# Fourier stage: own products in two halves, odd tokens' products on a summed tile, another order of the token tiles

## Chip, core and metric

The kernel runs on one core of a Trainium2 chip. The metric is the device time of one execution in microseconds (us), taken as the median of several runs. The engines are PE (TensorE, with PEld for its weight loads), DVE (VectorE), ACT (ScalarE), POOL (GpSimd) and SP (SyncE). In this trace each engine takes its own instructions in the order in which they stand (PE may load weights ahead), and they wait for one another by semaphores.

## The reference, cut to what matters

```python
def _attn_ref(q, k, v, proj):          # 2 x 8 heads x 768 tokens x 64
    mask = q_bucket[:, :, :, None] == k_bucket[:, :, None, :]
    ...
    return np.matmul(attn, v)
def _moe_ref(x, w_val, conv_w, w_out): # x: 2 x 768 x 512
    ...                                # gate: sigmoid of a 5-tap convolution along the tokens
    val = x @ w_val
    return gate * val @ w_out
def _moe2_ref(x, w_ch1, w_ch2):
    X = np.fft.fft(np.fft.fft(x, axis=1), axis=2)   # along tokens and along channels
    mixed = np.real(X)
    u = x + mixed
    un = (u - mu) / np.sqrt(var + 1e-06)            # layer norm over 512 channels
    ch = np.maximum(un @ w_ch1, 0.0) @ w_ch2        # 512 -> 2048 -> 512
    return u + ch
```

The change lies in the second half of `_moe_ref` (the product with `w_out`) and in the Fourier part of `_moe2_ref`.

## The kernel before

The program has three stages: attention (to about 245 us), the gated product and the Fourier part (`mixing`, to about 336 us), and the channel products (`channel`, to the end). The order of instructions on each engine is the order of the code: nothing is moved by a scheduler.

Each float32 number is split into a high and a low part of fewer bits, and a product is made of three: high by high, high by low, low by high. The Fourier part uses that a sequence of 768 splits into an even and an odd half of 384 (s = 0 and s = 1), each of three token tiles of 128 (kt = 0, 1, 2), for two batches b. That makes twelve jobs (b, s, kt). `mixing` is a software pipeline over rounds i = 0 to 13. In round i it runs

- `own` for job i: the product with `w_out`, 12 matmuls of 512 columns into one PSUM bank (4 channel blocks by 3 part products);
- `along_d` for job i-2: the transform along the channels, 6 matmuls of 258 columns for each part, then ACT writes the high part of the result into `ah` (tile `a` in the trace) and DVE the low part into `al`;
- `turn` for job i-1: two transposes, a copy on ACT (tile `ft`, high) and a subtraction on DVE (`ft`, low), which `along_d` of the next round reads;
- `fold` for job i: ACT copies the bank to a tile `y`, DVE folds it.

When all six jobs of a batch have gone through `along_d`, `both(b, kt)` runs `mixed` for s = 0 and 1 (the transform along the tokens: 9 matmuls of 258 columns over the three tiles, and then the odd tokens' extra products with the table `odd`), `total` (DVE adds the result to `y`) and two additions on GpSimd that give `u`. For batch 0 this stands in round 7, between `turn(6)` and round 8, for batch 1 behind round 13. The extra products are 2 for s = 0 (high and low of slot 3, of which row 0 alone counts), none for s = 1 with kt above 0, and 6 for s = 1 with kt = 0: the table's rows sum over all tokens, tile by tile, high and low. So a batch has 11 + 15 + 11 + 9 + 11 + 9 = 66 matmuls of 258 columns here.

Rounds 5 and 6 also hold the splitting of a 64-bit weight block for the channel stage (`channel_split`: DVE L146 to L157, ACT L149, L161, L169, GpSimd L162), rounds 8 to 10 the centering of `u[0]` (`center`), rounds 11 to 13 its transposes (`u_transpose`). The tiles `y` have seven buffers, so `fold` of job 7 waits until GpSimd has read a `y` of the first `both`.

Of the kernel before, what the change touches and what calls it, by code (L numbers as in the profile page):

```python
# [10 lines left out]
F32 = mybir.dt.float32  # L11
F32R = mybir.dt.float32r
AF = mybir.ActivationFunctionType
ALU = mybir.AluOpType
# [3 lines left out]
P = 128  # L18
B, H, S, D = 2, 8, 768, 64
DM = H * D  # L20
# [5 lines left out]
NC = DM // P  # L26
HS = S // 2
NL = 258
# [21 lines left out]
def dft_tables():  # L50


    d = np.arange(1, DM // 2 + 1)
    l = np.arange(NL)
    ang = 2.0 * np.pi * ((d[:, None] * l[None, :]) % DM) / DM
    cs = np.stack([np.cos(ang), np.sin(ang)], 0)
    cs[0, -1] = 0.5 - (l % 2)
    cs[1, -1] = 0.0
    ch, cl = split12(cs)
    wide = np.stack([ch, cl], 1).reshape(2, 2, 2, P, NL).transpose(3, 0, 1, 2, 4)  # L60

    j = np.arange(HS)
    k = np.arange(HS)
    ang = 2.0 * np.pi * ((j[:, None] * k[None, :]) % S) / S
    c = np.cos(ang)
    s = -np.sin(ang)
    c[0, 1::2] = 0.0
    c[1::2, 0] = 0.0
    s[:, 0] = 0.0
    t = 2.0 * np.stack([c, s], 0)  # L70
    th, tl = split12(t)
    seq = np.stack([th, tl], 1).reshape(2, 2, HS // P, P, HS).transpose(3, 0, 1, 2, 4)

    odd = np.zeros((P, 2, P), np.float32)
    odd[0, 0, 1::2] = 2.0
    odd[1::2, 1, 0] = 2.0
    return (
        np.ascontiguousarray(wide, dtype=np.float32),
        np.ascontiguousarray(seq, dtype=np.float32),
        odd,  # L80
    )
# [23 lines left out]
def block_kernel(  # L105
# [4 lines left out]
    nc = tc.nc  # L110

    def f32(ap):
        return ap.bitcast(F32)
# [922 lines left out]
    def u_transpose(b, t, psum):  # L1036
        pu = psum()
        for c in range(NC):
            nc.tensor.transpose(pu[:, c * P : (c + 1) * P], u[b][:, t, c * P : (c + 1) * P], ident)
        ts_ = slice(t * P, (t + 1) * P)  # L1040
        pv_ = pu.rearrange("p (c t) -> p c t", c=NC)
        nc.scalar.copy(uth[0][:, :, ts_], pv_)
        nc.vector.tensor_tensor(utl[0][:, :, ts_], pv_, f32(uth[0])[:, :, ts_], op=ALU.subtract)

    def mixing(es):
# [13 lines left out]
        gh, gl = {}, {}  # L1059
# [123 lines left out]

        def own(b, s, kt):
            yp = psum()
            n = 0
            for x, w in ((gh[b, s], wo_h), (gh[b, s], wo_l), (gl[b, s], wo_h)):
                for c in range(NC):
                    nc.tensor.matmul(  # L1189
                        yp, x[:, c, kt * P : (kt + 1) * P], w[c], start=n == 0, stop=n == 3 * NC - 1  # L1190
                    )
                    n += 1
            return yp

        ys, folds, turned = {}, {}, {}
# [23 lines left out]
        def along_d(b, s, kt, part):  # L1219
            fh, fl = turned[b, s, kt, part]  # L1220
            ops = [(x[:, i, :], tab[:, part, w, i, :]) for x, w in ((fh, 0), (fh, 1), (fl, 0)) for i in range(2)]
            pa = psum()
            for n, (x, w) in enumerate(ops):
                nc.tensor.matmul(pa[:, :NL], x, w, start=n == 0, stop=n == len(ops) - 1)  # L1224
            ah, al = sums[b]
            slot = kt if part == s else 3
            high, low = ah[:, part, slot, :], al[:, part, slot, :]
            if part:
                nc.scalar.copy(high, pa[:, :NL])
                nc.vector.tensor_tensor(low, pa[:, :NL], f32(high), op=ALU.subtract)  # L1230
            else:

                y0 = ys[b, s, kt][:, 0:1]
                nc.scalar.activation(high, pa[:, :NL], AF.Identity, bias=y0)
                nc.vector.scalar_tensor_tensor(
                    low, pa[:, :NL], y0, f32(high), op0=ALU.add, op1=ALU.subtract
                )

        def mixed(b, s, kt):
            ah, al = sums[b]  # L1240
            ks = slice(kt * P, (kt + 1) * P)
            ops = []
            for x, w in ((ah, 0), (ah, 1), (al, 0)):
                for jt in range(3):
                    ops.append((seq[:, s, w, jt, ks], x[:, s, jt, :]))
            if s == 0:
                ops += [(odd[:, 0, :], ah[:, 0, 3, :]), (odd[:, 0, :], al[:, 0, 3, :])]
            elif kt == 0:
                for jt in range(3):
                    ops += [(odd[:, 1, :], ah[:, 0, jt, :]), (odd[:, 1, :], al[:, 0, jt, :])]  # L1250
            pm = psum()
            for n, (w, x) in enumerate(ops):
                nc.tensor.matmul(pm[:, :NL], w, x, start=n == 0, stop=n == len(ops) - 1)  # L1253
            return pm
# [13 lines left out]
        def both(b, kt):  # L1268

            pm = [mixed(b, s, kt) for s in range(2)]  # L1270
            for s in range(2):
                total(b, s, kt, pm[s])
            for t, op in ((kt, ALU.add), (3 + kt, ALU.subtract)):
                nc.gpsimd.tensor_tensor(u[b][:, t, :], ys[b, 0, kt], ys[b, 1, kt], op=op)
# [14 lines left out]
        for i in range(len(jobs) + 2):  # L1289
            if i < len(jobs):  # L1290
                yp = own(*jobs[i])
            if i > 1:
                for x in spans(jobs[i - 2]):
                    if x[0] not in sums:
                        sums[x[0]] = [m2.tile([P, 2, 4, NL], F32R, tag=y, name="a") for y in ("ah", "al")]
                    along_d(*x)
            if 0 < i <= len(jobs):
                for x in spans(jobs[i - 1]):
                    turn(*x)
            if i == 7:  # L1300
                both(0, 0)
                both(0, 1)
            if i < len(jobs):
                fold(*jobs[i], yp)
            if i == 0:
                last_gates()
            elif i == 5:
                nc.scalar.activation(warm, warm, AF.Sqrt)
            if 0 < i < 5:
                for s in range(2):  # L1310
                    part_high(1, s, i - 1)
                    part_low(1, s, i - 1)
            if i < 4:
                even_odd(1, i)
            elif i == 4:
                gs.close()
                late_tiles()
                channel_load(0)
                channel_load(1)
            elif i == 7:  # L1320
                both(0, 2)
            elif 8 <= i < 11:
                for t in (i - 8, i - 5):
                    center(0, t)
            elif 5 <= i < 7:
                channel_split(i - 5)
            elif i > 10:
                for x in range(2):
                    u_transpose(0, 2 * (i - 11) + x, psum)
        wnext.extend(channel_steps(2, spare=False))  # L1330
        run(wnext.pop(0) for _ in range(3))
        both(1, 0)
        wnext.pop(0)()
        for kt in range(1, 3):
            both(1, kt)

    with ExitStack() as es:
# [127 lines left out]
```

## Time and profile before

| | us |
|---|---|
| median of 3 runs | 611.06 |
| lowest and highest | 610.6, 614.76 |
| the profiled execution's own time | 610.95 |
| its span | 609.1 |
| PE busy in the span | 600.7 |
| DVE, ACT, POOL busy | 441.4, 357.7, 265.3 |

The span is what the trace covers; the profiled execution's own time is 1.85 us longer. Rows of the trace give the start of an instruction, its duration, and for a matmul a modelled end. Consecutive matmuls overlap in the rows, so the pace of a stream is the distance of starts, not the duration of one.

### The profile page before, as it was taken

The numbers are of one execution on the slowest core, as the hardware profiler recorded it, in microseconds if no ns is written. First come the engines' busy times: TensorE is split into PE (matmuls) and PEld (weight loads), VectorE is DVE, ScalarE is ACT, GpSimd is POOL, SyncE is SP. The second block draws the span as 40 slices with busy tenths as digits, with TensorE's granted clock in tenths as the row PEclk, the third lists the DMA queues.
The fourth block names the chain that finished last, engine by engine and source line by source line (L and its number), as shares of the span: only waits on it lengthen the run. The fifth ranks groups of instructions, "written<-read, shape, count | busy, mean of one in ns | idle before, by whom it ended". The sixth has DMA issues, their size and how long they took to land.

```text
span 609.1 us, 10268 instructions
## 1 busy us (share of the span) xinstructions
PE 600.7 (99%) x3711; PEld 537.5 (88%) x3711; DVE 441.4 (72%) x849; ACT 357.7 (59%) x712; POOL 265.3 (44%) x274
## 2 busy tenths in 40 slices
PE   8999999999999999999999999999999999999997
PEld 7899999999999999998989888888888888888885
DVE  4999999999999997998679788988884411110113
ACT  5989999999999997745524455555665011111121
POOL 7251769788888798963341532332330000000000
PEclk9999999999999999999999999999999999999999
DMA  5967776878777712170200243443430200000002
GB/s 133 213 154 165 170 147 164 179 167 189 165 177 178 173 43 57 43 293 2 70 1 9 86 126 127 138 120 123 139 103 1 104 0 1 1 0 1 0 1 104
DMA packets 52556, 62.01 MB, mean 102 GB/s; under 512 B 28704, under 2 KB 39304, under 8 KB 52250
## 3 DMA queue, kind: packets, MB, share of 16 engines
q1 hardware_dynamic: 51770, 57.81, 37.3%
q0 software_dynamic: 432, 3.55, 1.5%
q8 instruction: 29, 0.48, 0.3%
q14 instruction: 21, 0.17, 0.1%
q10 hardware_dynamic: 304, 0.01, 0.0%
HBM read 36.73 MB, written 3.19 MB: 66 GB/s over the span
## 4 chain that ended last, share of the span: by engine, by line
PE 90%; DVE 6%; ACT 2%; issue 1%; DMA 1%; POOL 0%; SPq 0%; ACTq 0%; POOLq 0%
PE pf L1372 21%; PE acc L1382 20%; PE op L629 10%; PE sp L570 10%; PE ptp L606 9%; PE ps L1189 5%; PE ps L222 3%; PE ps L1253 3%; PE ps L1224 1%; PE bp L456 1%; PE late L222 1%; PE ptp L714 1%; PE early L222 1%; DVE ptl L618 1%; PE idle L369 1%
## 5 line engine op out<-in xcount | busy, mean ns | idle before, releaser
L1382 PE MATMUL acc<-w,hid 128*128 128x512 f32 x576 | 137.4, 391 | 0.0
L1382 PEld LDWEIGHTS acc<-w,hid 128*128 128x128 f32 x576 | 105.5, 188 | 20.1
L1375 DVE SCALAR_TENSOR_TENSOR hid<-pf,hid 128x512 fp32r<-128x512 f32 (+1 forms) x62 | 33.4, 556 | 120.6 <-ACT hid L1374 120.6
L1372 PE MATMUL pf<-uth,w 128*128 128x512 f32 (+1 forms) x496 | 97.2, 337 | 0.1
L1374 ACT ACTIVATE hid<-pf 128x512 fp32r<-128x512 f32 (+1 forms) x62 | 28.9, 488 | 114.9 <-PE pf L1372 114.9
L581 DVE TENSOR_SCALAR_CACHE_REDUCE sd<-sp 128x768 f32<-128x768 f32 x96 | 91.0, 948 | 4.8 <-PE sp L570 3.1
L618 DVE TENSOR_TENSOR ptl<-ptp,pth 128x768 fp32r<-128x768 f32 x96 | 91.5, 953 | 2.3 <-ACT pth L614 2.0
L570 PE MATMUL sp<-qk 128*128 128x512 f32 (+1 forms) x384 | 91.1, 359 | 1.7 <-DVE sd L581 0.8
L1372 PEld LDWEIGHTS pf<-uth,w 128*128 128x128 f32 x496 | 78.8, 188 | 15.6 <-DVE hid L1375 1.8
L588 ACT ACTIVATE sd<-sd,nm 128x768 f32<-128x768 f32 x96 | 90.5, 942 | 1.5 <-DVE sd L581 1.5
L614 ACT CAST pth<-ptp 128x768 fp32r<-128x768 f32 x96 | 77.4, 806 | 13.6 <-PE ptp L714 5.7
L162 POOL TENSOR_TENSOR w<-cv 128x512 fp32r<-128x512 f32 x31 | 40.4, 1302 | 89.0 <-DVE cv L157 74.5
L606 PE MATMUL ptp<-ident,sd 128*128 128x128 f32 x576 | 78.5, 272 | 0.2 <-ACT sd L588 0.2
L629 PE MATMUL op<-ptl,v 128*128 128x256 f32 x288 | 73.3, 284 | 0.2 <-DVE ptl L618 0.2
L629 PE MATMUL op<-pth,v 128*128 128x256 f32 x288 | 73.3, 282 | 0.0
L606 PEld LDWEIGHTS ptp<-ident,sd 128*128 128x128 f32 x576 | 65.8, 140 | 1.1 <-ACT sd L588 0.5
L570 PEld LDWEIGHTS sp<-qk 128*128 128x128 f32 x384 | 58.2, 189 | 8.3 <-DVE sd L581 1.6
L629 PEld LDWEIGHTS op<-pth,v 128*128 128x128 f32 x288 | 54.1, 188 | 4.1
L629 PEld LDWEIGHTS op<-ptl,v 128*128 128x128 f32 x288 | 54.1, 188 | 0.6 <-DVE ptl L618 0.4
L1372 PE MATMUL pf<-utl,w 128*128 128x512 f32 (+1 forms) x248 | 53.1, 335 | 0.0
L241 POOL TENSOR_TENSOR g<-g,conv_tmp 128x768 f32<-128x768 f32 x27 | 46.5, 1723 | 1.6
L149 ACT ACTIVATE cv<-cv,col 128x512 int32<-128x512 int32 x32 | 23.2, 725 | 40.4 <-DVE cv L146 40.4
(214 smaller groups left out, 984.2 us busy)
## 6 DMA issues: line engine op xcount, KB each, us to landing
raw<-in_moe_w_ch_dram SPq DMA_DIRECT2D x32, 512.0 KB
qk<-ht SPq DMA_DIRECT2D x60, 192.0 KB
qk<-lt SPq DMA_DIRECT2D x30, 192.0 KB
rqk<-in_q_dram SPq DMA_DIRECT2D x16, 192.0 KB
rqk<-in_k_dram SPq DMA_DIRECT2D x16, 192.0 KB
rv<-in_v_dram SPq DMA_DIRECT2D x8, 384.0 KB
out_dram<-o SPq DMA_DIRECT2D x12, 256.0 KB
xm<-xc SPq DMA_DIRECT2D x15, 192.0 KB
```

The costliest lines, as they stand in the source:

```text
L162: nc.gpsimd.tensor_tensor(dst()[1], fold(g.bitcast(F32)), fold(e.bitcast(F32)), op=ALU.mult)
L241: nc.gpsimd.tensor_tensor(dst, dst, tmp, op=ALU.add)
L570: nc.tensor.matmul(sp[:, cs], q2[i][:, m, qi * P : (qi + 1) * P], k2[i][:, m, cs], start=m == order[0], stop=m == order[1])
L581: nc.vector.tensor_scalar(sd[n], sp, CLAMP, None, op0=ALU.min, op1=ALU.min, accum_out=st[p]["nm"][:, n % 12 : n % 12 + 1],)
L588: nc.scalar.activation(sd[n], sd[n], AF.Exp, bias=st[p]["nm"][:, i : i + 1], scale=-1.0, accum_out=st[p]["sums"][:, i : i + 1],)
L606: nc.tensor.transpose(tp[:, r // 3, c0 : c0 + P], sd[n][:, r * P : (r + 1) * P], ident)
L614: nc.scalar.copy(p_parts(n)[0], tp)
L618: nc.vector.tensor_tensor(lo, tp, f32(ho), op=ALU.subtract)
L629: nc.tensor.matmul(po[kb], v3[:, r, c0 : c0 + P], pt[kb][x][:, r, :], start=r == 0 and x == 0, stop=r == R - 1 and x == 1,)
L1372: nc.tensor.matmul(pf, w[:, c, :], x[:, c, cs], start=n == 0, stop=n == 3 * NC - 1)
L1375: nc.vector.scalar_tensor_tensor(hl[:, cs], pf, 0.0, f32(hh)[:, cs], op0=ALU.max, op1=ALU.subtract)
L1382: nc.tensor.matmul(acc, x[:, ts_], w, start=f == 0 and n == 0, stop=f == NF - 1 and n == 2)
```

## The change

- `own` makes its bank in two halves of 256 columns, each a group of 12 matmuls: 24 matmuls where 12 were. `fold` still waits for the whole.
- For s = 0 the extra products are one matmul instead of two: DVE writes the low part of row 0 to row 32 of the high tile's slot 3, and the table `odd` has a second row of twos there.
- For s = 1 and kt = 0 they are two instead of six: GpSimd adds the high and low tiles of s = 0 over kt into `tot` (three additions behind `along_d` of kt = 1, two behind that of kt = 2), ACT copies the sum into the high tile's unused slot, and GpSimd subtracts to get its low part.
- `both` runs in the order kt = 1, 2, 0, and `center` and `u_transpose` of batch 0 follow that order.

```diff
+    odd[32, 0, 1::2] = 2.0
...
         def own(b, s, kt):
             yp = psum()
-            n = 0
-            for x, w in ((gh[b, s], wo_h), (gh[b, s], wo_l), (gl[b, s], wo_h)):
-                for c in range(NC):
-                    nc.tensor.matmul(
-                        yp, x[:, c, kt * P : (kt + 1) * P], w[c], start=n == 0, stop=n == 3 * NC - 1
-                    )
-                    n += 1
+            for c0 in range(0, DM, 2 * P):
+                n = 0
+                for x, w in ((gh[b, s], wo_h), (gh[b, s], wo_l), (gl[b, s], wo_h)):
+                    for c in range(NC):
+                        nc.tensor.matmul(
+                            yp[:, c0 : c0 + 2 * P], x[:, c, kt * P : (kt + 1) * P], w[c][:, c0 : c0 + 2 * P],
+                            start=n == 0, stop=n == 3 * NC - 1,
+                        )
+                        n += 1
             return yp
...
+                rows = slice(0, 1 if s else P)
                 nc.vector.scalar_tensor_tensor(
-                    low, pa[:, :NL], y0, f32(high), op0=ALU.add, op1=ALU.subtract
+                    high[32:33] if s else low, pa[rows, :NL], y0[rows], f32(high)[rows], op0=ALU.add, op1=ALU.subtract
                 )
+                if s == 0 and kt:
+                    all_tokens(b, kt)
+
+        tokens = {}
+
+        def all_tokens(b, kt):
+            ah, al = (f32(x) for x in sums[b])
+            oh = sums[b][0][:, 1, 3, :]
+            if kt == 1:
+                tokens[b] = m2.tile([P, NL], F32, tag="tot", name="tot")
+            t = tokens[b]
+            add = [ah[:, 0, kt, :], al[:, 0, kt, :]]
+            if kt == 1:
+                add.append(al[:, 0, 0, :])
+            for n, x in enumerate(add):
+                nc.gpsimd.tensor_tensor(t, ah[:, 0, 0, :] if kt == 1 and n == 0 else t, x, op=ALU.add)
+            if kt == 2:
+                nc.scalar.copy(oh, t)
+                nc.gpsimd.tensor_tensor(sums[b][1][:, 1, 3, :], t, f32(oh), op=ALU.subtract)
...
             if s == 0:
-                ops += [(odd[:, 0, :], ah[:, 0, 3, :]), (odd[:, 0, :], al[:, 0, 3, :])]
+                ops.append((odd[:, 0, :], ah[:, 0, 3, :]))
             elif kt == 0:
-                for jt in range(3):
-                    ops += [(odd[:, 1, :], ah[:, 0, jt, :]), (odd[:, 1, :], al[:, 0, jt, :])]
+                ops += [(odd[:, 1, :], x[:, 1, 3, :]) for x in (ah, al)]
...
             if i == 7:
-                both(0, 0)
                 both(0, 1)
+                both(0, 2)
...
             elif i == 7:
-                both(0, 2)
+                both(0, 0)
...
-                for t in (i - 8, i - 5):
+                for t in ((i - 7) % 3, (i - 7) % 3 + 3):
                     center(0, t)
...
-                    u_transpose(0, 2 * (i - 11) + x, psum)
+                    u_transpose(0, (1, 4, 2, 5, 0, 3)[2 * (i - 11) + x], psum)
...
-        both(1, 0)
+        both(1, 1)
         wnext.pop(0)()
-        for kt in range(1, 3):
+        for kt in (2, 0):
             both(1, kt)
```

Lines after the change carry other numbers: L1214 is then L1217, L1199 is L1202, L1229 is L1232, L1234 is L1237, L149, L161, L162 and L169 one more each.

ACT in rounds 6 and 7 of the kernel before, from the high part of job 4 to that of job 5 (`a` high part, `ft` the turned tile of job 5, `y` job 6, `cv` and `w` the split of a weight block):

```order
L1234 ACTIVATE a<-ps,y 128x258 [waits PE_49,Activation_49]
L1214 CAST ft<-pw 128x256 [waits PE_49]
L1199 COPY y<-ps 128x512
L149 ACTIVATE cv<-cv,col 128x512 [waits DVE_49,Activation_49]
L161 ACTIVATE cv<-cv 128x512 [waits DVE_49,Pool_49]
L169 CAST w_0_4176<-cv 128x512 [waits DVE_49]
L1229 CAST a<-ps 128x258 [waits PE_49]
```

The same stretch of ACT in the changed kernel:

```order
L1237 ACTIVATE a<-ps,y 128x258 [waits PE_49,Activation_49]
L1259 CAST a<-tot 128x258 [waits Pool_49]
L1217 CAST ft<-pw 128x256 [waits PE_49]
L1202 COPY y<-ps 128x512
L150 ACTIVATE cv<-cv,col 128x512 [waits DVE_49,Activation_49]
L162 ACTIVATE cv<-cv 128x512 [waits DVE_49]
L170 CAST w_0_4240<-cv 128x512 [waits DVE_49]
L1232 CAST a<-ps 128x258 [waits PE_49]
```

The copy of the sum, which waits for GpSimd, now stands ahead of the copy of `ft` and of all that follows; in round 12 it stands in the same way between the high part of job 10 and the copy of `ft` of job 11.

POOL in rounds 4 to 7 of the kernel before, from the last pair of low parts of the gated tiles (`gl`) to the first `u`:

```order
L1090 TENSOR_TENSOR gl<-gt_3963,gh 128x384 [waits Activation_49]
L1090 TENSOR_TENSOR gl<-gt_3964,gh 128x384 [waits Activation_49]
L162 TENSOR_TENSOR w_0_4175<-cv 128x512 [waits DVE_49,Activation_49]
L162 TENSOR_TENSOR w_0_4177<-cv 128x512 [waits DVE_49,PE_49,Activation_49]
L1274 TENSOR_TENSOR u_4161<-y 128x512 [waits DVE_49]
```

The same stretch of POOL in the changed kernel:

```order
L1257 TENSOR_TENSOR tot<-tot,a 128x258 [waits DVE_49,Pool_49]
L1257 TENSOR_TENSOR tot<-tot,a 128x258 [waits Pool_49]
L1091 TENSOR_TENSOR gl<-gt_3963,gh 128x384 [waits Activation_49]
L1091 TENSOR_TENSOR gl<-gt_3964,gh 128x384 [waits Activation_49]
L163 TENSOR_TENSOR w_0_4239<-cv 128x512 [waits DVE_49,Activation_49]
L1257 TENSOR_TENSOR tot<-tot,a 128x258 [waits Activation_49,Pool_49]
L1257 TENSOR_TENSOR tot<-tot,a 128x258 [waits DVE_49,Pool_49]
L1260 TENSOR_TENSOR a<-tot,a 128x258 [waits DMAHW5_49,Activation_49]
L163 TENSOR_TENSOR w_0_4241<-cv 128x512 [waits DVE_49,PE_49,Activation_49]
```

The additions of kt = 1 stand ahead of the last `gl` pair, those of kt = 2 behind the first weight block of the channel stage, and the subtraction behind ACT's copy.

## Rows read from the trace of the kernel before

**Rows 1.** The page: its first line, and busy time by engine (share, instructions).

```profile
span 609.1 us, 10268 instructions
PE 600.7 (99%) x3711; PEld 537.5 (88%) x3711; DVE 441.4 (72%) x849; ACT 357.7 (59%) x712; POOL 265.3 (44%) x274
```

**Rows 2.** The page's chain that ended last, shares of the span by engine.

```profile
PE 90%; DVE 6%; ACT 2%; issue 1%; DMA 1%; POOL 0%; SPq 0%; ACTq 0%; POOLq 0%
```

**Rows 3.** Windows: stretch, length, then PE, PEld, DVE, ACT, POOL busy, clock.

```profile
320.00:330.00 10.00, 9.85 (x74) 9.06 (x73) 9.73 (x23) 5.77 (x15) 0.00 (x0) 1.00 0.00 1
```

**Rows 4.** Chain in order of time: start, length, piece, instructions.

```profile
269.79 5.61 PE ps L1189 x24
...
299.02 8.21 PE ps L1253 x66
...
328.06 7.95 PE ps L1253 x66
```

**Rows 5.** Timeline of PE, channel stage: start, duration, line, shapes, count.

```profile
487.88 1.08 PE L1372 MATMUL pf<-uth,w 128*128 128x256 f32 x8
488.79 0.62 PE L1372 MATMUL pf<-utl,w 128*128 128x256 f32 x4
489.25 4.26 PE L1382 MATMUL acc<-w,hid 128*128 128x512 f32 x18
```

**Rows 6.** Chain in the attention stage: groups of six 256-column matmuls.

```profile
62.68 0.70 PE op L629 x6
```

**Rows 7.** The page's groups: weight loads of the channel stage's first product.

```profile
L1372 PEld LDWEIGHTS pf<-uth,w 128*128 128x128 f32 x496 | 78.8, 188 | 15.6 <-DVE hid L1375 1.8
```

**Rows 8.** Timeline of PE, round 7 and the first `both`.

```profile
297.92 0.88 PE L1224 MATMUL ps<-tab,ft 128*128 128x258 f32 x6
298.64 0.38 PE L1209 MATMUL pw<-ident,fold 128*128 128x128 f32 x2
298.78 1.33 PE L1253 MATMUL ps<-a,seq 128*128 128x258 f32 x9
...
300.19 1.49 PE L1253 MATMUL ps<-a,seq 128*128 128x258 f32 x9
...
307.06 2.01 PE L1189 MATMUL ps<-qk,gh 128*128 128x512 f32 x8
```

**Rows 9.** Timeline of ACT, rounds 6 and 7, and round 12.

```profile
295.91 0.47 ACT L1234 ACTIVATE a<-ps,y 128x258 fp32r<-128x258 f32 x1
296.28 0.36 ACT L1214 CAST ft<-pw 128x256 fp32r<-128x256 f32 x1
296.53 0.60 ACT L1199 COPY y<-ps 128x512 f32<-128x512 f32 x1
...
300.14 0.37 ACT L1229 CAST a<-ps 128x258 fp32r<-128x258 f32 x1
...
324.94 0.49 ACT L1234 ACTIVATE a<-ps,y 128x258 fp32r<-128x258 f32 x1
325.32 0.38 ACT L1214 CAST ft<-pw 128x256 fp32r<-128x256 f32 x1
```

**Rows 10.** Timeline of POOL, rounds 4 to 6.

```profile
289.39 1.98 POOL L1090 TENSOR_TENSOR gl<-gt,gh 128x384 fp32r<-128x384 f32 x2 [1.90 <-ACT gh L1087]
295.95 1.29 POOL L162 TENSOR_TENSOR w<-cv 128x512 fp32r<-128x512 f32 x1 [4.59 <-DVE cv L157]
```

**Rows 11.** Timeline of PE, round 13: `along_d` of job 11.

```profile
325.80 0.72 PE L1224 MATMUL ps<-tab,ft 128*128 128x258 f32 x4
326.68 0.51 PE L1224 MATMUL ps<-tab,ft 128*128 128x258 f32 x2 [0.15 <-DVE ft L1215]
```

**Rows 12.** Timeline of DVE: the fold of round 6, the low part in round 12.

```profile
297.16 0.42 DVE L1202 TENSOR_TENSOR fold<-ps,y 128x256 f32<-128x256 f32 x1
...
325.81 0.48 DVE L1235 SCALAR_TENSOR_TENSOR a<-ps,y,a 128x258 fp32r<-128x258 f32 x1
```

## The prediction, made before the changed kernel was run

> **What bounds the kernel now.** I read the page's first lines, then the chain that ended last, then windows and timelines of the stretch that the change touches. The page [rows 1] shows PE busy for 600.7 of 609.1 us, and the chain [rows 2] puts 90% of the span on PE. In the Fourier stage PE starts one matmul behind another without a gap that counts: even in the window from 320 to 330 us, where DVE is nearly full as well, PE is busy 9.85 of 10 us, at full granted clock [rows 3]. So in this stage two things move the end: how long PE's streams take, and any wait that is put into them. GpSimd is idle in that window, and all that the change gives it lies beside PE, unless somebody waits for it. Who waits is the question of this prediction.
>
> **Streams on PE: own products.** The chain gives 5.61 us for 24 matmuls of 512 columns [rows 4], 233.8 ns each and 2.805 us for a bank. No row shows these products in halves. The nearest is the channel stage's first product, which also runs twelve matmuls of 256 columns with new weights each into one bank: they start at 487.88 us, the next stream at 489.25 [rows 5], so 1.37 us for twelve and 114 ns each. Two halves are then 2.74 us, 0.065 us less than one whole. Over twelve banks that is 12 x 0.065 = 0.78 us gained. Other rows bound it from the other side: six matmuls of 256 columns in attention take 0.70 us [rows 6], 117 ns each, and a bank 2.80 us, so nothing gained; 66 matmuls of 258 columns take 7.95 us [rows 4], 120.5 ns each, and at that pace a bank costs 2.89 us, 0.085 us more, 1.0 us lost in all. I take the row of the channel stage, whose twelve steps into one bank are the same form, and keep 1.0 us lost as the other end.
>
> The Trainium skill, "TensorE: Matmul & The Clock Gate", section "Back-to-back issue gap", gives 262 cycles for 256 columns and 518 for 512 at full clock: by it two halves cost 6 cycles, 2.5 ns, more than a whole, 0.36 us over 144 pairs, where the rows above give 228 against 234 ns. It speaks against the change, and by it the sum below would be 1.1 us higher. The trace does not bear out its pace for the whole (216 ns against 234 ns).
>
> **Streams on PE: odd tokens.** For each batch s = 0 drops one matmul for each of three tiles, and s = 1 drops four: seven of 120.5 ns, 0.84 us, 1.69 us for both. These stand in the middle of the stream and all of it is PE's path. The changed order of tiles adds and removes no matmul; the transposes and the centering only follow it. The single-row write to row 32 replaces a DVE instruction of the same length along the columns; I cost it at nothing, since DVE's instruction stays in its place.
>
> If nothing waited, the sum would be 0.78 + 1.69 = 2.47 us gained.
>
> **What GpSimd's additions cost by themselves.** Two pairs of rows bound one addition of 258 columns: 384 columns take 1.98 / 2 = 0.99 us, 512 columns 1.29 us [rows 10]. The straight line through both gives 0.70 us for 258, in proportion to columns it would be 0.67; 0.99 is the upper end. I take 0.71. The three behind kt = 1 are waited for by nobody soon: GpSimd idles 1.90 us ahead of the `gl` pair [rows 10], so they push that pair by at most one addition, and the banks of batch 1 read it last among their part products. I cost them at nothing; if that cover were gone it would be one addition, 0.7 us, once.
>
> **The new wait, batch 0.** The copy of the sum stands in ACT's queue ahead of the copy of `ft` of job 5, and waits for GpSimd. Behind it are queued, in this order, the copy of `ft`, the copy `y` of job 6, three steps of a weight block's split, and the high part of job 5. In the kernel before ACT began the high part of job 4 at 295.91, `ft` at 296.28, `y` at 296.53, the high part of job 5 at 300.14 [rows 9]. PE began `along_d` of job 5, which reads `ft`, at 297.92 [rows 8]: it had the copy (0.36 us long) 1.3 us ahead.
>
> Now the steps, by the clock of the kernel before. Six banks come ahead of round 6, so all is 6 x 0.065 = 0.39 us earlier there. GpSimd ends the weight block at 295.95 + 1.29 - 0.39 = 296.85 [rows 10] and only then begins the first addition; two end at 298.27. ACT's copy starts at 298.29, `ft` 0.25 us behind it (the distance between `ft` and `y` in the rows) at 298.54, and is done 0.37 us later, at 298.91. PE is there at 297.92 - 8 x 0.065 = 297.40. **First wait: 1.5 us.** `along_d` lasts 0.72 us (297.92 to 298.64 [rows 8]), to 299.63. Meanwhile `y` starts at 298.79, 2.26 us later than before, and with it the fold of job 6, which ends at 297.16 + 0.42 + 2.26 = 299.84 [rows 12]: 0.2 us more until PE's transposes. They take 0.14 us; then ten matmuls for s = 0 and two for s = 1, 12 x 0.1205, bring PE to 301.43. The third one for s = 1 reads the high part of job 5, which stands behind the split in ACT's queue: the whole chain fold, DVE's split steps, ACT's split steps is 2.26 us later, so it is ready at 300.14 + 2.26 + 0.37 = 302.77. **Second wait: 1.35 us.** From there 7 + 19 + 21 = 47 matmuls, 5.66 us, end at 308.43, where the next bank starts. In the kernel before it started at 307.06 [rows 8]. So batch 0 is 1.37 us later: waits of 1.5 + 0.2 + 1.35 = 3.05, less 0.52 of eight banks, 0.84 of odd tokens, and 0.3 that the mixing lost before (8.28 us from 298.78 to 307.06 for 66 x 0.1205 = 7.95 [rows 4, 8]).
>
> The second `both` now mixes kt = 2 before job 7's fold can have its `y`, but no bank or tile runs out for PE by the order of the changed kernel: the fold would be done at about 309, and its transposes come behind the next bank and `along_d`, at about 312.
>
> **Between.** Four banks, 4 x 0.065 = 0.26 us, earlier.
>
> **The new wait, batch 1.** In round 12 the same copy stands between the high part of job 10 (324.94) and `ft` of job 11 (325.32) [rows 9]. GpSimd is idle there, so the first addition starts at once and ends at 324.94 + 0.49 + 0.71 = 326.14; the second needs DVE's low part, done at 325.81 + 0.48 = 326.29 [rows 12], and ends at 327.01. Copy at 327.03, `ft` at 327.28, done at 327.66, where PE began `along_d` of job 11 at 325.80 and its last two at 326.68 [rows 11]. It would end at 327.66 + 0.72 = 328.38 in place of 326.68 + 2 x 0.12 = 326.92. **Third wait: 1.46 us** more than before. Against it stand the 0.84 us of odd tokens: 0.62 us later at the end of the mixing. GpSimd's subtraction (0.71 us behind ACT's copy) is read by the last matmul of the mixing, some 8 us later, and hidden. The channel stage begins with weights and `u` that were ready before, and DVE's totals keep their distance to PE, so I carry the delay through to the end.
>
> **Sum.** 1.37 - 0.26 + 0.62 = 1.73 us later, against the profiled execution's own time of 610.95, 0.11 us under the median: 612.7 us. The gain of 2.47 us is more than paid back by 4.5 us of waits, less 0.3 that goes away.
>
> **Rivals.** *The gain is had.* ACT's wait is hidden, because GpSimd is sooner done than I price it or PE has other work. For it: GpSimd is idle in batch 1 and PE waits for nearly nothing now. Against it: in round 12 `ft` was done at 325.70 and PE began at 325.80, so a delay of over 0.1 us shows, and in round 6 (done at 296.65, begun at 297.92) one of over 1.3 us. Then 2.47 us are gained: 608.5 us. Chance 0.18.
>
> *Halves cost more than wholes.* At 120.5 ns a bank costs 0.085 us more in place of 0.065 less, 12 x 0.15 = 1.8 us: 614.5 us, and with additions of 0.99 us (two in each of two waits, the first counted twice, 0.28 x 2 + 0.28 = 0.85 us) 615.4. It decides from 117 ns a matmul on, and is slower than before on any count. For it: the rows of 258 columns. Against it: twelve in a row at 114 ns. Chance 0.17.
>
> *Weight loads set the pace of halves.* One load lasts 188 ns [rows 7], and halves need 288 of them, 54.1 us where 144 wholes took 33.7. If a load stopped hiding behind a matmul of 256 columns, 20.4 us would come on top: 633 us, slower by over 3%. It decides where the pace goes over 117 ns towards 188. Against it: the channel stage's 256-column products need the same load for each matmul and run at 114 ns. Chance 0.03.
>
> *The change does nothing*, waits and gains cancelling within 0.5 us: part of the forecast's lower end, 611 us; chance 0.04.
>
> **How the numbers follow.** My forecast, three waits against two gains, has 0.58: 612.7 us. The range must take in the gain that is had and the dear halves, since each alone has almost 0.2: from 608.4 to 615.4 us. What a measurement of this kernel can tell from no change is about 1%, 6.1 us. Only the weight loads, and noise beyond what three runs show, reach that: slower by over 1% 0.04, faster by over 1% 0.02, within it 0.94.
>
> **What would show it.** In the profile after, ACT should show a wait of some 2 us ahead of the copy of the sum in rounds 6 and 12, released by GpSimd; PE should show waits of about 1.5 us ahead of `along_d` of jobs 5 and 11 and about 1.3 us in the first `mixed` for s = 1, where the kernel before has 0.15 us in job 11 [rows 11] and none that counts elsewhere. A bank of own products should take 2.74 us. The extra products should leave 59 matmuls of 258 columns in each mixing. PE's waits absent, or a bank at 2.8 us or more, would each show a step wrong; a granted clock under full behind one of the waits would make all of it wrong.

## The result, and the profile after

The changed kernel takes 615.5 us (median of 19 runs, 614.1 to 618.23), the kernel before 611.1 us (19 runs). The ratio is 1.0071, with a 95% interval from 1.0061 to 1.0081: 4.4 us slower, where 1.7 us were forecast. The profiled execution took 615.5 us.

The page of the kernel after, first lines (against [rows 1]):

```profile
span 613.7 us, 10546 instructions
PE 600.9 (98%) x3841; PEld 543.3 (89%) x3841; DVE 441.8 (72%) x849; ACT 358.8 (58%) x714; POOL 273.6 (45%) x286
```

PE's busy time is the same and the span 4.6 us longer, though 14 matmuls of 258 columns are gone. First the queue of ACT and GpSimd's work, from the timeline of the kernel after (start, duration, engine, line, operation, shapes, count, idle time before it and its releaser; against [rows 9, 10]):

```profile
295.90 0.47 ACT L1237 ACTIVATE a<-ps,y 128x258 fp32r<-128x258 f32 x1
295.95 1.29 POOL L163 TENSOR_TENSOR w<-cv 128x512 fp32r<-128x512 f32 x1 [3.54 <-DVE cv L158]
297.20 1.55 POOL L1257 TENSOR_TENSOR tot<-tot,a 128x258 f32<-128x258 f32 x2
298.78 0.41 ACT L1259 CAST a<-tot 128x258 fp32r<-128x258 f32 x1 [2.41 <-POOL tot L1257]
299.09 0.36 ACT L1217 CAST ft<-pw 128x256 fp32r<-128x256 f32 x1
...
327.11 0.48 ACT L1237 ACTIVATE a<-ps,y 128x258 fp32r<-128x258 f32 x1
329.29 0.41 ACT L1259 CAST a<-tot 128x258 fp32r<-128x258 f32 x1 [1.71 <-POOL tot L1257]
329.61 0.36 ACT L1217 CAST ft<-pw 128x256 fp32r<-128x256 f32 x1
```

ACT stands 2.41 us in round 6 and 1.71 us in round 12 until GpSimd has its sum, with `ft` behind it, as predicted. An addition takes 0.77 us (predicted 0.71). PE pays for it, in the same timeline (against [rows 8, 11]):

```profile
297.32 0.62 PE L1191 MATMUL ps<-qk,gl 128*128 128x256 f32 x4
299.51 0.98 PE L1227 MATMUL ps<-tab,ft 128*128 128x258 f32 x6 [1.57 <-ACT ft L1217]
300.55 0.41 PE L1212 MATMUL pw<-ident,fold 128*128 128x128 f32 x2
300.71 1.33 PE L1275 MATMUL ps<-a,seq 128*128 128x258 f32 x9
...
303.37 2.19 PE L1275 MATMUL ps<-a,seq 128*128 128x258 f32 x16 [0.97 <-ACT a L1232]
...
309.12 1.09 PE L1191 MATMUL ps<-qk,gh 128*128 128x256 f32 x8
...
330.02 1.18 PE L1227 MATMUL ps<-tab,ft 128*128 128x258 f32 x6 [1.81 <-ACT ft L1217]
331.00 1.91 PE L1040 MATMUL ps<-ident,u 128*128 128x128 f32 x8
332.56 1.99 PE L1275 MATMUL ps<-a,seq 128*128 128x258 f32 x9
```

The three waits are there: 1.57, 0.97 and 1.81 us. The last two rows show something more. Nine matmuls of 258 columns that took 1.33 us at 300.71 take 1.99 us at 332.56. Windows of the kernel after (columns as in [rows 3]; the clock is the number after the busy times):

```profile
328.00:330.00 2.00, 0.21 (x2) 0.00 (x0) 0.37 (x1) 0.71 (x3) 1.41 (x3) 1.00 0.00 0
330.00:331.00 1.00, 0.98 (x6) 0.98 (x7) 0.93 (x2) 0.94 (x2) 0.42 (x1) 0.82 0.03 8
331.00:332.00 1.00, 1.00 (x6) 1.00 (x6) 1.00 (x3) 0.37 (x1) 0.00 (x0) 0.50 0.00 0
332.00:333.00 1.00, 1.00 (x7) 1.00 (x6) 0.40 (x2) 0.64 (x2) 0.00 (x0) 0.50 0.00 0
333.00:334.00 1.00, 1.00 (x7) 1.00 (x7) 0.84 (x2) 0.53 (x1) 0.00 (x0) 0.50 0.00 0
334.00:336.00 2.00, 2.00 (x18) 2.00 (x18) 1.97 (x6) 0.73 (x1) 0.00 (x0) 0.99 0.00 0
```

Behind the wait, in which PE was busy 0.21 of 2 us, the granted clock falls to 0.50, that is 1.2 GHz, for a little over 3 us. The prediction named this only as something that would make it wrong.

An own product in halves, from the timeline of the kernel after (against [rows 4, 5]):

```profile
279.45 1.17 PE L1191 MATMUL ps<-qk,gh 128*128 128x256 f32 x8
280.46 0.62 PE L1191 MATMUL ps<-qk,gl 128*128 128x256 f32 x4
280.91 1.07 PE L1191 MATMUL ps<-qk,gh 128*128 128x256 f32 x8
281.82 0.62 PE L1191 MATMUL ps<-qk,gl 128*128 128x256 f32 x4
282.27 1.59 PE L1227 MATMUL ps<-tab,ft 128*128 128x258 f32 x12
```

The second half runs from 280.91 to 282.27, 1.36 us, the predicted 1.37. The first half, behind transposes, takes 1.46 us. Together that is 2.82 us; the prediction named 2.8 or more as a sign that a step was wrong.

**Where the time lies, for all kernels.** The stage can be cut at three starts of PE's streams: the first own product of job 0, that of job 8, and the channel stage's first product. B0 is the stretch from the first to the second, B1 from the second to the third, C from the third to the channel stage's first product of its third hidden block. Each is a difference of two rows of that kernel's timeline; for the kernel before they start at 269.63, 307.06, 335.85 and 348.29 us, for the changed one at 269.76, 309.12, 340.38 and 352.83. The sums are those of one profiled execution each, the medians those of all runs. The ratio compares runs of the two kernels that were taken together, so it is not the quotient of the medians in the table.

| kernel | B0 | B1 | C | sum | median us | ratio to before, interval |
|---|---|---|---|---|---|---|
| before | 37.43 | 28.79 | 12.44 | 78.66 | 611.1 | |
| after | 39.36 | 31.26 | 12.45 | 83.07 | 615.5 | 1.0071 (1.0061 to 1.0081) |
| e1 both copies late | 37.65 | 27.93 | 13.24 | 78.82 | 610.71 | 1.0003 (0.999 to 1.0016) |
| e2 before with halves | 37.27 | 28.63 | 12.51 | 78.41 | 610.91 | 0.9999 (0.9988 to 1.001) |
| e3 after with wholes | 39.52 | 31.25 | 12.60 | 83.37 | 615.52 | 1.0069 (1.0057 to 1.0081) |
| e4 one filler | 39.86 | 29.62 | 13.14 | 82.62 | 615.19 | 1.0069 (1.0056 to 1.0082) |
| e6 late in batch 0 | 37.52 | 29.59 | 13.14 | 80.25 | 613.5 | 1.0038 (1.0024 to 1.0052) |
| e7 late in batch 1 | 39.84 | 27.94 | 13.22 | 81.00 | 613.37 | 1.0035 (1.0022 to 1.0048) |
| e8 e1, additions late | 36.58 | 27.93 | 13.23 | 77.74 | 610.25 | 0.9983 (0.9974 to 0.9991) |
| e9 e8, one addition on VectorE | 36.55 | 27.83 | 13.53 | 77.91 | 610.4 | 0.9993 (0.9985 to 1.0002) |
| e10 e8, one addition left out | 36.64 | 27.83 | 12.43 | 76.90 | 609.12 | 0.9971 (0.9959 to 0.9983) |
| e11 two fillers | 39.51 | 29.59 | 13.17 | 82.27 | 614.59 | 1.0062 (1.0049 to 1.0074) |
| e12 first part alone | 37.14 | 28.25 | 12.69 | 78.08 | 610.25 | 0.9992 (0.9981 to 1.0004) |
| e13 copy on GpSimd | 37.94 | 27.85 | 13.14 | 78.93 | 611.35 | 1.0005 (0.9995 to 1.0015) |

Median less sum is 531.9 to 532.6 us in every row but e6 (533.3), whose profiled execution ran at full clock (612.64 us, 0.9 under its median; its two runs at a mean clock of 0.997 took 614.3 and 614.4). So the three stretches hold what the kernels differ by. Two profiled executions lost time ahead of these stretches, where their code is that of the changed kernel: that of e1 took 614.57 us, 3.9 over its median, with the granted clock between 0.50 and 0.72 from 243 to 247 us, and that of e11 took 616.5 us, 1.9 over its median, with a wait of PE of 2.02 us for a DMA at 39.62 us.

### The profile page after: what moved, and what is told of

Read it like the earlier page. It is cut to its first block, busy times and chain, and to the rows that moved or that the text cites. A ratio compares the mean times of both kernels' runs of the same rounds, so it can differ in the third digit from the quotient of the medians.

```text
span 613.7 us, 10546 instructions
## 1 busy us (share of the span) xinstructions
PE 600.9 (98%) x3841; PEld 543.3 (89%) x3841; DVE 441.8 (72%) x849; ACT 358.8 (58%) x714; POOL 273.6 (45%) x286
## 4 chain that ended last, share of the span: by engine, by line
PE 92%; DVE 4%; ACT 2%; issue 1%; POOL 1%; POOLq 0%
PE pf L1394 21%; PE acc L1404 21%; PE op L630 11%; PE sp L571 11%; PE ptp L607 10%; PE ps L1191 5%; PE ps L223 3%; PE ps L1275 2%; PE ps L1227 1%; PE bp L457 1%; PE late L223 1%; PE ptp L715 1%; PE early L223 1%; DVE sd L582 1%; DVE ptl L619 1%
```

## The experiments

My theory behind the result: ACT's copy of the sum holds up ACT's queue, PE waits for `ft`, and the clock falls behind the wait. Rivals: the halves are slow, or the sum itself is late for its readers, or the lower clock costs nothing.

### Undoing one part each: e1, e2, e3, e4

e1 takes the copy and the subtraction out of `all_tokens` into `token_parts`:

```diff
-            if kt == 2:
-                nc.scalar.copy(oh, t)
-                nc.gpsimd.tensor_tensor(sums[b][1][:, 1, 3, :], t, f32(oh), op=ALU.subtract)
...
             if i == 7:
+                token_parts(0)
                 both(0, 1)
...
+        token_parts(1)
         wnext.extend(channel_steps(2, spare=False))
```

> The changed kernel, but ACT's copy of the sum and GpSimd's subtraction stand later: for batch 0 ahead of the first mixing in round 7, for batch 1 behind round 13. Theory (the copy's place in ACT's queue makes PE wait, and the third wait takes TensorE's clock down to 0.50 for some 3.4 us): PE's waits of 1.57, 0.97 and 1.81 us and the low clock all go, so 3.0 us come back in batch 0 and 3.7 in batch 1, 615.5 - 6.7 = 608.8 to 609.9 us, 0.2 to 0.4% under the kernel before. Rival (the additions on GpSimd or the order of the tiles are dear by themselves and the wait only moves, to DVE or to the mixing's last matmul): 612 us or more, with new waits of PE of over 0.5 us each.

610.71 us: 4.8 us come back, all the change had lost, but it is more than the 608.8 to 609.9 us expected. PE no longer waits for `ft`, and its clock is full in both mixings. But the gain of some 2 us that this leaves does not come. Two rows of the table say where it goes: B0 is 0.2 us over before, and C is 0.8 us longer. In round 7 the second wait is still there (timeline of e1):

```profile
300.63 1.63 POOL L1257 TENSOR_TENSOR tot<-tot,a 128x258 f32<-128x258 f32 x2
300.93 0.73 DVE L147 TENSOR_SCALAR cv<-raw 128x512 int32<-128x512 int32 x1
301.58 0.96 DVE L153 TENSOR_SCALAR cv<-raw 128x512 int32<-128x512 int32 x1
...
304.85 2.20 PE L1281 MATMUL ps<-a,seq 128*128 128x258 f32 x16 [1.08 <-ACT a L1232]
```

DVE's two steps of the weight block's split take 0.73 and 0.96 us beside GpSimd's additions; ACT's split steps wait for them, and the high part of job 5 stands behind these in ACT's queue.

e2 is the kernel before with `own` in halves, e3 the changed kernel with `own` in wholes.

> The kernel before with the own products in two halves and nothing else. Theory from the trace after (a bank in halves takes 2.84 us against 2.80): 12 x 0.04 = 0.5 us slower, 611.6 us. The prediction's term (2.74 us a bank): 0.78 us faster, 610.3 us. Both are within 0.15% of the kernel before, so the distance from one bank's start to the next stream's start in the profile decides, 2.82 or more against 2.74.

> The changed kernel with own products in one piece of 512 columns again; all else as changed. Theory (halves cost 0.04 us a bank; waits and the low clock are the copy's): 615.0 us, the waits of PE within 0.3 us of those of the changed kernel, clock 0.50 again behind the third. Prediction's term: 616.3 us. Rival (the halves bring about the low clock): no stretch at 0.50 and about 613.5 us.

e2: 0.16 us less in B0 and in B1, 0.3 us in all, and nothing that shows in the median. e3: the waits are 1.44, 0.98 and 1.82 us, the clock falls again, and the time is that of the changed kernel. The halves are not the cause, and they are worth less than half of what was predicted.

e4 puts work that nobody reads into the third wait:

```diff
+            if i == 13:
+                spare = bank()
+                for _ in range(14):
+                    nc.tensor.matmul(spare[:, : 2 * P], seq[:, 0, 0, 0, :P], tab[:, 0, 0, 0, : 2 * P], start=True, stop=True)
             if i > 1:
                 for x in spans(jobs[i - 2]):
```

> The changed kernel with 14 matmuls of 256 columns that nobody reads, ahead of the channel transform of job 11 in round 13, where PE waits 1.8 us for ACT; they write a spare bank and add work, the output stays the same. Theory (the clock fell because PE stood idle there): PE starts that transform at the same distance as in the changed kernel, but at clock 1.00, and the 1.7 us that the stretch at 0.50 cost come back: 613.8 us. Rival (the clock falls there for another reason, or the fall costs nothing since DVE is as late): 615.5 us, unchanged.

615.19 us where 613.8 were expected. It is inconclusive alone: the clock is full in batch 1 (B1 1.64 us shorter), but in this execution it fell behind the first wait, of 1.58 us, in place of the third (0.50 from 301 to 304 us), and C is 0.7 us longer.

### One batch at a time: e6, e7

`token_parts` of e1 for batch 0 alone, and for batch 1 alone.

> The copy and the subtraction of the sum come later in batch 0 only (ahead of the first mixing of round 7); batch 1 stays as changed. Theory (each batch pays for its own wait on ACT's copy): TensorE's wait of 1.57 us ahead of along_d of job 5 goes, a wait of about 1 us in the first mixed for s = 1 stays, as in the kernel with both copies late, and the third wait of 1.8 us with the clock at 0.50 behind it stays: 613.4 to 614.0 us. Rival (the clock falls because of all waits together, and recovers when one of them is gone): batch 1 runs at full clock too, 612 us or less.

> The copy and the subtraction come later in batch 1 only (behind round 13); batch 0 stays as changed. Theory: the waits of 1.57 and 0.97 us stay, the third wait and the clock's fall behind it go, and 0.8 us are lost again where the channel stage begins, since VectorE is then the later engine: 612.4 to 613.0 us. Together with the other single batch this should add up to the kernel with both late (4.8 us under the changed kernel). Rival (the fall of the clock costs nothing in the end, since VectorE is late anyway): only the wait of 1.8 us less 0.8 comes back, 614.5 us; second rival: the clock falls behind the wait of batch 0 in place of batch 1, as in the run with the filler, 613.5 us or more.

613.5 and 613.37 us: 2.0 and 2.1 us back, together 4.1 of e1's 4.8. Each batch pays for its own wait. The clock did not do what was expected in either. Of e6's six runs three took 612.1 to 612.7 us, and in its profiled execution the same wait of 1.81 us did not bring the clock down. So e6 gives the price of the clock (timeline and one window):

```profile
328.00 0.98 PE L1227 MATMUL ps<-tab,ft 128*128 128x258 f32 x6 [1.81 <-ACT ft L1217]
328.82 1.03 PE L1040 MATMUL ps<-ident,u 128*128 128x128 f32 x8
329.61 1.33 PE L1281 MATMUL ps<-a,seq 128*128 128x258 f32 x9
```

```profile
330.00:332.00 2.00, 2.00 (x19) 2.00 (x19) 2.00 (x5) 0.80 (x3) 0.00 (x0) 1.00 0.00 0
```

B1 is 29.59 us there and 31.26 in the changed kernel's profile: the fall costs 1.67 us of the stretch. e7 came out over the 612.4 to 613.0 us expected, because in it the clock fell in batch 0, as in e4 (0.59, 0.50, 0.50 and 0.70 in the four us from 301). The wait of 0.97 us was then gone, because PE came later to it, and B0 is only 0.5 us longer than in the changed kernel.

### Fillers in both waits: e11

As e4, with `if i in (7, 13)`.

> The changed kernel with 14 matmuls of 256 columns, which nobody reads, ahead of along_d of job 5 and of job 11. The two places where TensorE waits for ACT's copy are filled with work, so that the waits' length stays and TensorE is not idle in them. Theory (the fall of the granted clock stands behind these two idle stretches and costs about 1 us of the time): full clock in both mixings, 614.4 to 614.8 us. Rival (the lower clock is hidden, since what TensorE waits for in either mixing comes no earlier): 615.2 to 615.5 us, as with one filler.

614.59 us, 0.9 us under the changed kernel. The clock is full in both mixings (window of e11):

```profile
296.00:340.00 44.00, 42.78 (x357) 41.89 (x356) 33.22 (x78) 16.86 (x38) 18.59 (x19) 1.00 0.09 26
```

PE begins `along_d` of job 5 and of job 11 no earlier: 29.86 us behind the first own product and 20.80 us behind that of job 8, against 29.75 and 20.90 us in the changed kernel. So the fall's net price is 0.9 us here: 1.67 us less the 0.7 us by which C is longer when PE comes earlier. The size is not sharp. The intervals of the two ratios overlap, and of the nineteen runs of the changed kernel the six with a mean clock of 0.999 or 1.0 have a median of 614.9 us, the seven at 0.997, among them the profiled one, 615.4, the six at 0.993 and 0.994 616.1: 0.5 us for the first step.

That the fall goes with these two waits shows in the runs as well: a mean clock of 0.997 or less stands in 13 of the nineteen, but in none of e11's six and in none of the eleven each of e8 and e13, where PE does not wait for `ft`.

### Who makes PE wait: e13

```diff
-                nc.scalar.copy(oh, t)
+                nc.gpsimd.tensor_copy(oh, t)
```

> The changed kernel with the copy of the sum made by GpSimd, which also makes the sum, in place of ACT; every other instruction stays in its place. Theory (the sum itself is early enough; what costs is that ACT's queue stands behind it): the waits of 1.57 and 1.81 us and the fall of the clock go, GpSimd's work beside VectorE's split leaves a wait of 1 to 1.7 us in round 7, and 0.7 us are lost where the channel stage begins: 610.7 to 611.4 us. Rival (the sum is too late for its readers on TensorE, whoever copies it): the waits move to the last odd-token products, 613 us or more.

611.35 us. One instruction on another engine, nothing moved, and 4.2 us are back. The sum is in time for PE; what cost the time was the queue behind ACT's copy. The wait in round 7 is longer than in e1, since GpSimd now has two more operations beside DVE's split (timeline of e13):

```profile
297.36 0.89 PE L1227 MATMUL ps<-tab,ft 128*128 128x258 f32 x6
298.48 0.48 POOL L1259 CAST a<-tot 128x258 fp32r<-128x258 f32 x1
...
301.53 2.19 PE L1275 MATMUL ps<-a,seq 128*128 128x258 f32 x16 [1.62 <-ACT a L1232]
```

### What holds back the rest: e8, e9, e10

e8 is e1 with batch 0's two additions of kt = 2 in round 7 as well:

```diff
-                if s == 0 and kt:
+                if s == 0 and (kt == 1 or kt and b):
                     all_tokens(b, kt)
...
             if i == 7:
+                all_tokens(0, 2)
                 token_parts(0)
```

> Both copies late, and in batch 0 GpSimd's two additions of kt = 2 come later as well, in round 7 behind its part of the weight block. Theory (the wait of 1.08 us in the first mixed for s = 1 stands there because VectorE's two tensor-scalar steps of the split take 0.73 and 0.96 us beside GpSimd's additions in place of 0.42 each): the two steps take 0.42 us again, the wait falls to 0.3 us or less, 609.7 to 610.0 us. Rival (the wait is that of the weight block's split as such, which the removed matmuls no longer cover): the wait stays near 1 us and the time at 610.7 us.

610.25 us, a little over what was expected, and 0.17% under the kernel before, with an interval that excludes 1: this version beats both. The steps are short again and the wait is nearly gone (timeline of e8):

```profile
296.75 0.42 DVE L147 TENSOR_SCALAR cv<-raw 128x512 int32<-128x512 int32 x1
297.08 0.42 DVE L153 TENSOR_SCALAR cv<-raw 128x512 int32<-128x512 int32 x1
299.82 2.20 PE L1281 MATMUL ps<-a,seq 128*128 128x258 f32 x16 [0.24 <-ACT a L1232]
...
334.42 5.81 POOL L1302 TENSOR_TENSOR u<-y 128x512 f32<-128x512 f32 x4 [0.25 <-DVE y L1292]
338.99 1.53 DVE L153 TENSOR_SCALAR cv<-raw 128x512 int32<-128x512 int32 x1
343.78 3.02 PE L1413 MATMUL acc<-w,hid 128*128 128x512 f32 x12 [0.38 <-DVE hid L1406]
```

The last three rows are C: a step of 0.42 us lasts 1.53 us, until GpSimd is done with the additions to `u` (334.42 + 5.81 = 340.23), and PE waits 0.38 us for the `hid` behind it. e9 gives one of these additions to DVE, e10 leaves it out:

```diff
             for t, op in ((kt, ALU.add), (3 + kt, ALU.subtract)):
-                nc.gpsimd.tensor_tensor(u[b][:, t, :], ys[b, 0, kt], ys[b, 1, kt], op=op)
+                e = nc.vector if (b, t) == (1, 3) else nc.gpsimd     # e9; e10: skipped for (1, 3)
+                e.tensor_tensor(u[b][:, t, :], ys[b, 0, kt], ys[b, 1, kt], op=op)
```

> As the one before, and the last of GpSimd's six additions to u of batch 1 (tile 3) is made by VectorE, behind its totals. Theory (the 0.8 us lost where the channel stage begins come from the tensor-scalar step of 1.52 us that runs beside GpSimd's additions): that step takes 0.42 us again, VectorE has a gap ahead of hid in which its own addition of 0.7 us lies, TensorE's wait of 0.38 us and the late hid go: 0.8 us less than the kernel before it in this list, 608.9 to 609.2 us. Rival (VectorE is the bound there and work given to it costs its own length): 0 to 0.7 us more than the kernel before it.

> As the kernel with both copies and batch 0's two additions late, and without the last of GpSimd's six additions to u of batch 1: token tile 3 of batch 1 is left out and set to zero in round 4, so this part of the output is not computed. Theory (the 0.7 to 0.8 us lost where the channel stage begins come from VectorE's tensor-scalar step that stands 1.53 us beside GpSimd's additions): GpSimd is done 1.4 us earlier, the step takes 0.5 us or less, and the stretch from the channel stage's first stream to the third one's is 12.5 us again in place of 13.2: 609.5 us. Rival (VectorE's own work is the bound there, because the mixing is shorter by its odd tokens and VectorE's totals are not): the stretch stays at 13.2 us and the time at 610.2 us.

e10: C is 12.43 us again and the time 609.12 us, 1.1 us under e8. In e10 the step takes 0.42 us again, behind GpSimd's last addition (timeline of e10):

```profile
335.11 4.31 POOL L1304 TENSOR_TENSOR u<-y 128x512 f32<-128x512 f32 x3 [0.24 <-DVE y L1292]
339.69 0.42 DVE L153 TENSOR_SCALAR cv<-raw 128x512 int32<-128x512 int32 x1
```

So GpSimd's additions are the cause of C's 0.8 us, and DVE's own work is not. e9 missed: DVE's addition and the step behind it, L165, which took 0.67 us in e8, each ran 1.75 us or more beside GpSimd's remaining ones, and PE waited for the weight block in place of `hid` (timeline of e9):

```profile
335.03 4.23 POOL L1303 TENSOR_TENSOR u<-y 128x512 f32<-128x512 f32 x3 [0.25 <-DVE y L1292]
336.36 1.75 DVE L1303 TENSOR_TENSOR u<-y 128x512 f32<-128x512 f32 x1
338.04 1.78 DVE L165 SCALAR_TENSOR_TENSOR w<-cv 128x512 fp32r<-128x512 int32 x1
339.87 1.20 PE L1404 MATMUL acc<-uth,w 128*128 128x512 f32 x4 [0.47 <-DVE w L165]
```

### The change without the sum: e12

```diff
-                if s == 0 and kt:
-                    all_tokens(b, kt)
...
-                ops += [(odd[:, 1, :], x[:, 1, 3, :]) for x in (ah, al)]
+                for jt in range(3):
+                    ops += [(odd[:, 1, :], ah[:, 0, jt, :]), (odd[:, 1, :], al[:, 0, jt, :])]
```

> The changed kernel without the sum: the tile with both parts (the low part's row written to row 32) serves s = 0, whose three matmuls a batch are saved, the halves and the order of token tiles stay, and s = 1 takes its six odd-token matmuls in tile 0 as before. Nothing is made by GpSimd for it. Theory (all that went wrong hangs on the sum): no wait over 0.2 us, six matmuls of 0.12 us saved, 0.3 us of the halves, less 0.3 to 0.4 us given back where the channel stage begins: 610.3 to 610.7 us. Rival (the changed order of the tiles has a cost of its own): 611.2 us or more.

610.25 us, as expected (its ratio, paired with runs of before, is 0.9992 and does not exclude 1). The tile with both parts, the halves and the order of the token tiles cost nothing that shows (PE's longest wait in the mixings is 0.23 us); the waits and the falls of the clock hang on the sum. C is 0.25 us longer than before even so. e12 saves three matmuls a batch without GpSimd and stands level with e8, which saves seven.

## Why the prediction was wrong

The direction and the mechanism of the waits were right, the size was off by 2.7 us. Three steps failed: the clock's fall has no term in the sum, the halves were mis-sized, and the path from the mixing into the channel stage was put at nothing. Step by step:

- **The waits** were right in place and cause, and near in size: PE was to come 1.5, 1.35 and 1.86 us too early and waited 1.57, 0.97 and 1.81 us. The second was 0.4 us shorter. The third entered the sum with 1.46 us and costs 1.66 at full clock (B1 of e6 less that of e1). `along_d` of job 5 itself takes 0.3 us longer (1.04 us from 299.51 to 300.55), since DVE's low part of `ft` comes late too; 0.2 us was counted there, for the fold. e13 and e1 show the copy in ACT's queue as the cause.
- **Odd tokens** were right: the mixing of batch 1 takes 7.17 us in e1 (331.39 to 338.56) and took 8.03 before (327.82 to 335.85), 0.86 us less where 0.84 were predicted.
- **Own halves** were mis-sized: 0.065 us a bank predicted, 0.32 / 12 = 0.03 us measured in e2. Both of its prices were low. The whole was read from the first two banks; by the distances of starts the twelve take 34.36 us in the kernel before, 2.86 each, and 33.97 us, 2.83 each, in e2. The row of the channel stage [rows 5] was of twelve products behind another such block; that is the pace of the second half (1.36 us), and the first half, behind transposes, takes 1.46. This is 0.46 us of the error.
- **Batch 0, +1.37 us** with the 0.52 of eight banks counted in, came out as 39.36 - 37.43 = 1.93 us. Beside the halves, the 0.3 us that the mixing lost before were written off as gained; the 59 matmuls take 309.12 - 300.71 = 8.41 us, which is 0.97 of wait and 0.33 over their 7.11. The shorter second wait makes up for that. What is left is mostly the halves, 0.52 counted and 0.16 measured in B0 of e2.
- **Batch 1, -0.26 + 0.62 = +0.36 us,** would be +0.80 us at full clock (e6). With the clock's fall it is 31.26 - 28.79 = +2.47 us. The fall, 1.67 us of it, is the largest part of the error, and it has no term in the sum.
- **"I carry the delay through to the end"** holds in the changed kernel's profile (C 12.45 against 12.44) only because the clock fell. At full clock C is 0.7 us longer (13.14 in e6, 13.17 in e11), a term that was put at nothing. It is the step of DVE's split that meets the last of GpSimd's additions to `u`: 1.53 us in e8 and 1.42 in e6, but 0.76 in the changed kernel, where PE is slowed and the step begins later against the additions.

0.56 us in B0, 0.44 in B1 without the clock and 1.67 from it make 2.67 us, and 1.73 + 2.67 = 4.4 us is the result. But without the fall the 0.7 us of C would stand in its place: at full clock the changed kernel would take about 614.6 us (e11), still 1.9 over the forecast.

Of the rivals, "the gain is had" fell with the waits. The dear halves fell too: halves gain 0.3 us in e2, and e3 is as slow with wholes, so that their 615.4 us lies near the result by chance. The weight loads fell with them. What stays open: why the same wait brings the clock down in one execution and not in another, and in one batch rather than in the other. The wait alone does not decide it: e13's of 1.62 us in round 7 and the DMA's of 2.02 us in e11 left the clock at 1.00.

## What to carry to other kernels

A copy that waits for a slow engine costs what stands behind it in its own engine's queue: look for that first, and put the copy where its result is needed, or on the engine that makes the operand. A wait on PE can have a second price, the lower clock behind it, as in most runs of the changed kernel; it belongs in the sum as a term with a chance, not only in the list of what could go wrong. Matmuls that are saved next to a stage in which VectorE and GpSimd work side by side came back here only as far as those two were off the path: of the 2.0 us of PE's streams that the change saves (1.69 and 0.32), e8 keeps 0.9 (78.66 less 77.74).

## What the hardware showed beyond that

DVE's steps depend on what GpSimd does at the time. A tensor-scalar step of 512 columns took 0.42 us alone and 0.73 to 1.53 us where it met GpSimd's additions, and an addition of two SBUF tiles on DVE 1.75 us. The split's L165 took 0.67 us in e8 and 1.78 in e9, with GpSimd's additions running in both; the totals, which read PSUM, kept their 0.41 us beside the same additions. Which of the two began first decided who paid. In e8 L165 began just ahead of an addition, and the addition took 1.82 us where the one before it took 1.29 (timeline of e8):

```profile
335.65 0.67 DVE L165 SCALAR_TENSOR_TENSOR w<-cv 128x512 fp32r<-128x512 int32 x1
335.67 1.82 POOL L1302 TENSOR_TENSOR u<-y 128x512 f32<-128x512 f32 x1
```

In e9 L165 began at 338.04, behind an addition that ran from 337.52 to 339.26, and paid itself. The Trainium skill, "SBUF — State Buffer", section "Who interferes with whom", says that the two engines share a pair of ports, that whichever starts first holds it for its whole instruction, and that on VectorE's side only certain forms and instructions with two SBUF inputs need it; the traces agree, with the numbers above.

The granted clock fell to 0.50 behind a wait of 1.8 us in the changed kernel and in e3, and stayed at 1.00 behind the same wait in e6; behind the wait of 1.6 us in batch 0 it fell in e4 and e7 and stayed at 1.00 in the changed kernel. With 14 matmuls in both waits it stayed at 1.00 (e11).
